# A smaller descriptor scratch for dynamic DMAs in an attention and mixture-of-experts kernel

## Chip, core and metric

The kernel runs on one core of one Trainium2 chip. The metric is the time of one execution in device microseconds (us). Times of several runs are given as the median with the lowest and highest.

## What is computed

The reference chains three parts:

```python
scores = scale * q @ k.T                      # 4 batches, 8 heads, 576 tokens, 64 wide
attn = (scores * Dmat) @ v                    # Dmat: gamma[h] ** (i - j) for i >= j, else 0
x = attn as [2304 tokens, 512]
# layer 1: top-1 mixture of 8 experts, each with room for `capacity` tokens
e = argmax(x @ w_gate); g = softmax(x @ w_gate)[e]
x2 = g * (relu(x @ w1[e]) @ w2[e])            # 512 -> 1024 -> 512; 0 where the expert is full
# layer 2: only tokens with x2 @ w_skip > 0 go through a second mixture of 8 experts
out = x2 + (g2 * (relu(x2 @ w1b[e2]) @ w2b[e2]) if x2 @ w_skip > 0 else 0)
```

All data is float32.

## The kernel before

Attention runs first, in 20 units (4 batches, 4 pairs of heads and one unit for the tail of each batch). Its output is written to a table of rows `xd` in device memory, 128 tokens at a time, by plain transfers issued from ScalarE. Routing (argmax, gate, rank of each token in its expert) is done on VectorE and TensorE while attention still runs.

The two expert layers each go through nine positions: eight experts in order of their size, the largest split in two. A position has a fixed number of token slots (`CAPS`), in tiles of 128. For each position `gather_rows` (line 838) fetches the token rows into SBUF by an indirect transfer per tile of 128 rows, from `xd` in layer 1 and from `x2d` in layer 2. `transposes` (line 704) turns them with TensorE into tiles named x_0T to x_8T, and eight steps of matmuls follow (`s1`, lines 727 to 734; `s2`, lines 753 to 768). Weights come by plain transfers from SyncE, in quarters of an expert, and where a position has more than 192 slots ScalarE (line 673) and VectorE (line 674) split them into a high and a low part.

After a position `post1` or `post2` turns the result back into rows. Layer 1 writes the rows to `x2d` (plain, from ScalarE) and scatters those that skip layer 2 to `out` (`scatter`, line 845); layer 2 scatters all its rows to `out`, adding the gathered row on VectorE (line 914). Rows of empty slots get an index beyond the table and are left out. GpSimd issues every gather and every scatter, and nothing else that is dynamic; its instructions stand in an order written out by hand: `run` asks for the gather of position p + 2 in step 6 of position p, and the scatters of a position come after it. The first gathers of a layer can't come so early, since their indices or rows are not ready.

The memory of a stage is given out in pools that are opened and closed in the code: those for attention close before the ones that only the expert layers need (`gr` for gathered rows, `xp`, `yp`) are opened. [...]

## Times and profile before

| | |
|---|---|
| median of 3 runs | 584.06 us (583.22 to 586.92) |
| the profiled execution | 584.51 us, its span 582.6 us |
| mean granted TensorE clock | 0.982 of full speed |
| TensorE matmuls / weight loads busy | 550.9 us / 513.8 us |
| VectorE, ScalarE, GpSimd busy | 309.7, 226.3, 144.8 us |
| DMA | 116.20 MB in 116085 packets |

The profile is one execution of the program. Its span is the time from the first to the last instruction; the time of the execution is 1.9 us longer. An engine's busy time is the sum over its instructions. L838 means line 838 of the kernel. PE is TensorE, PEld its weight loads, DVE VectorE, ACT ScalarE, POOL GpSimd, SP SyncE; a q behind an engine is its sequencer. [...]

### The profile page before, as it was taken

What the parts mean: (1) busy time and instruction counts of PE and PEld (TensorE: products, weight loads), DVE (VectorE), ACT (ScalarE), POOL (GpSimd) and SP (SyncE); (2) the same over time, 40 slices, a digit from 0 to 9 for tenths busy, and PEclk for the clock granted to TensorE, in tenths of its full rate; (3) what the DMA queues carried; (4) which work ended last, traced back from release to release, by engine and by line L of the source; (5) the groups of instructions that cost most, each with busy time, mean ns of one, the idle gap of its engine ahead of it and who ended that gap; (6) DMA issues with size and microseconds to landing.
All of it is one profiled execution on the core that took longest, in us unless ns stands there. A gap on an engine that the chain in (4) does not pass through costs nothing.

```text
span 582.6 us, 12184 instructions
## 1 busy us (share of the span) xinstructions
PE 550.9 (95%) x4545; PEld 513.8 (88%) x4545; DVE 309.7 (53%) x926; ACT 226.3 (39%) x457; POOL 144.8 (25%) x192
## 2 busy tenths in 40 slices
PE   5999989999899999999999999879999999999991
PEld 5989879788899999999999999768998999999980
DVE  4767889445365756767676767695556201110110
ACT  2343444413444545455455555534443222112110
POOL 4355362012221140405040304050204112210110
PEclk7899999999999999999999999989999999999997
DMA  8869786187875474655465556367646378788860
GB/s 193 188 177 252 200 252 241 42 270 224 285 258 195 155 244 156 206 176 187 162 215 154 187 169 206 123 199 232 220 129 204 131 247 257 224 278 262 259 210 9
DMA packets 116085, 116.20 MB, mean 199 GB/s; under 512 B 47654, under 2 KB 88870, under 8 KB 116018
## 3 DMA queue, kind: packets, MB, share of 16 engines
q1 hardware_dynamic: 104432, 90.12, 50.8%
q0 software_dynamic: 6320, 15.74, 8.4%
q10 hardware_dynamic: 5266, 9.48, 4.4%
q8 instruction: 38, 0.62, 0.4%
q14 instruction: 29, 0.24, 0.1%
HBM read 101.11 MB, written 17.92 MB: 204 GB/s over the span
## 4 chain that ended last, share of the span: by engine, by line
PE 81%; DVE 8%; DMA 5%; SPq 1%; issue 1%; POOL 1%; ACT 1%; POOLq 0%; DVEq 0%
PE h L727 10%; PE y L763 9%; PE h L732 6%; PE h L734 6%; PE h L733 6%; PE y L767 6%; PE y L768 5%; PE y L766 5%; PE S L187 3%; PE O L229 3%; PE O L223 2%; PE yr L797 2%; PE y L755 1%; PE Tk L170 1%; PE y L756 1%; PE y L757 1%
## 5 line engine op out<-in xcount | busy, mean ns | idle before, releaser
L674 DVE TENSOR_TENSOR lo<-r,hi 128x1024 fp32r<-128x1024 f32 x80 | 97.9, 1224 | 65.2 <-ACT hi L673 63.3
L673 ACT CAST hi<-r 128x1024 fp32r<-128x1024 f32 x80 | 83.9, 1049 | 66.2 <-PE y L767 28.3
L767 PE MATMUL y<-hl,hi 128*128 128x316 f32 (+7 forms) x256 | 76.4, 300 | 0.9 <-DVE hl L738 0.8
L768 PE MATMUL y<-hh,lo 128*128 128x316 f32 (+7 forms) x256 | 75.9, 298 | 0.0
L766 PE MATMUL y<-hh,hi 128*128 128x316 f32 (+7 forms) x256 | 73.3, 298 | 0.0
L763 PE MATMUL y<-hh,r 128*128 128x168 f32 (+3 forms) x448 | 71.6, 302 | 1.6 <-ACT hh L729 1.6
L763 PEld LDWEIGHTS y<-hh,r 128*128 128x128 f32 x448 | 64.6, 190 | 2.0 <-ACT hh L729 1.8
L737 ACT ACTIVATE hh<-h 128x240 fp32r<-128x240 f32 (+8 forms) x80 | 32.1, 401 | 71.9 <-PE h L734 70.1
L785 DVE COPY yt<-y 128x168 f32<-128x168 f32 (+11 forms) x30 | 11.8, 395 | 89.0 <-ACT yt L787 64.4
L729 ACT ACTIVATE hh<-h 128x168 f32<-128x168 f32 (+4 forms) x64 | 19.3, 302 | 95.7 <-PE h L727 95.4
L845 POOL DMA_INDIRECT out<-o,six x18 | 19.2, 1065 | 144.7 <-DVE o L914 142.6
L738 DVE SCALAR_TENSOR_TENSOR hl<-h,hh 128x240 fp32r<-128x240 f32 (+8 forms) x80 | 35.4, 443 | 31.6 <-ACT hh L737 31.6
L767 PEld LDWEIGHTS y<-hl,hi 128*128 128x128 f32 x256 | 48.2, 188 | 2.1 <-DVE hl L738 1.9
L768 PEld LDWEIGHTS y<-hh,lo 128*128 128x128 f32 x256 | 48.2, 188 | 0.0
L766 PEld LDWEIGHTS y<-hh,hi 128*128 128x128 f32 x256 | 47.1, 188 | 0.1
L845 POOL DMA_INDIRECT out<-x2r,si x24 | 27.8, 1158 | 10.4 <-issue 6.0
L190 DVE TENSOR_TENSOR P<-S,tab 128x512 f32<-128x512 f32 (+1 forms) x40 | 23.7, 631 | 11.2 <-PE S L187 10.9
L838 POOL DMA_INDIRECT g<-xd,gix x20 | 23.9, 1194 | 9.4 <-issue 5.8
L154 POOL TENSOR_TENSOR vh<-v,tab 128x512 f32<-128x512 f32 x15 | 16.2, 1082 | 26.3 <-PE O L229 17.2
L207 DVE TENSOR_TENSOR st<-st,kv 64x64 f32<-64x64 f32 x96 | 20.9, 218 | 3.0
L797 PE MATMUL yr<-ident,yt 128*128 128x128 f32 (+11 forms) x148 | 21.9, 280 | 0.5 <-DVE o L914 0.5
L187 PE MATMUL S<-qT,kT 64*128 64x128 f32 x288 | 22.4, 295 | 0.0
(757 smaller groups left out, 1288.4 us busy)
## 6 DMA issues: line engine op xcount, KB each, us to landing
r<-w1a SPq DMA_DIRECT2D x36, 512.0 KB, 4.8
r<-w2a SPq DMA_DIRECT2D x36, 512.0 KB, 4.0
r<-w1b SPq DMA_DIRECT2D x36, 512.0 KB, 5.5
r<-w2b SPq DMA_DIRECT2D x36, 512.0 KB, 4.0
xd<-xr ACTq DMA_DIRECT2D x18, 256.0 KB, 3.9
k<-k SPq DMA_DIRECT2D x32, 128.0 KB, 3.3
q<-q SPq DMA_DIRECT2D x16, 256.0 KB, 3.8
v<-v SPq DMA_DIRECT2D x32, 128.0 KB, 4.1
```

Source lines behind the costliest of these rows:

```text
L187: nc.tensor.matmul(S[hh][:, c], s.kT[hp, cs], s.qT[hp, cs], start=True, stop=True)
L673: nc.scalar.copy(hi, raw)
L674: nc.vector.tensor_sub(lo, raw, hi.bitcast(F32))
L727: nc.tensor.matmul(ps, w.r1[:, c, fc], s.xh[:, c, 0:C], start=(c == 0), stop=(c == 3))
L732: nc.tensor.matmul(ps, w.hi1[:, c, fc], s.xh[:, c, 0:C], start=(c == 0), stop=False)
L733: nc.tensor.matmul(ps, w.hi1[:, c, fc], s.xl[:, c, 0:C], start=False, stop=False)
L738: nc.vector.scalar_tensor_tensor(out=s.hl[f], in0=ps, scalar=0.0, in1=s.hh[f].bitcast(F32), op0=ALU.max, op1=ALU.subtract)
L763: nc.tensor.matmul(y, w.r2[:, f % 2, dc], s.hh[f], start=a, stop=o)
L766: nc.tensor.matmul(y, wh, s.hh[f], start=a, stop=False)
L767: nc.tensor.matmul(y, wh, s.hl[f], start=False, stop=False)
L768: nc.tensor.matmul(y, wl, s.hh[f], start=False, stop=o)
L845: r = g.nc.gpsimd.indirect_dma_start(out=g.oa["out"][:, :], out_offset=IndirectOffsetOnAxis(ap=idx, axis=0), in_=rows, in_offset=None, bou ...
```

## The change

The program is built with an explicit size of the scratch for descriptors, 4096 bytes a partition. Nothing else is touched.

```diff
-    nc = bacc.Bacc("TRN2", target_bir_lowering=False, num_devices=1)
+    nc = bacc.Bacc("TRN2", target_bir_lowering=False, num_devices=1, dynamic_dma_scratch_size=4096)
```

## Rows read from the trace of the kernel before

**Rows 1.** The page's first part: busy us, share of the span, instructions.
```profile
PE 550.9 (95%) x4545; PEld 513.8 (88%) x4545; DVE 309.7 (53%) x926; ACT 226.3 (39%) x457; POOL 144.8 (25%) x192
```

**Rows 2.** The chain of waits that ended last, shares by engine.
```profile
PE 81%; DVE 8%; DMA 5%; SPq 1%; issue 1%; POOL 1%; ACT 1%; POOLq 0%; DVEq 0%
```

**Rows 3.** TensorE's waits: for what, us in total, times, longest us.
```profile
PE s8I L466 <- DVE s8B L460: 3.0, 1, 3.0
...
PE x_1T L704 <- DMA g<-xd,fx: 1.7, 1, 1.7
...
PE x_0T L704 <- DMA g<-x2d,fx: 0.9, 1, 0.9
```

**Rows 4.** DMA queues: packets, MB, share of 16 engines; the software queue.
```profile
q0 software_dynamic: 6320, 15.74, 8.4%
```

**Rows 5.** Groups of GpSimd's instructions: count | busy us, mean ns | idle before.
```profile
L845 POOL DMA_INDIRECT out<-x2r,si x24 | 27.8, 1158 | 10.4 <-issue 6.0 <-ACT hh L737 2.6 <-ACT hi L673 1.8
L838 POOL DMA_INDIRECT g<-xd,gix x20 | 23.9, 1194 | 9.4 <-issue 5.8 <-DVE lv1lim L558 3.6
L845 POOL DMA_INDIRECT out<-o,six x18 | 19.2, 1065 | 144.7 <-DVE o L914 142.6 <-issue 2.1
L838 POOL DMA_INDIRECT g<-x2d,gix x16 | 17.8, 1110 | 6.8 <-issue 3.0 <-DVE gix L593 2.2 <-PE h L727 0.6
...
L838 POOL DMA_INDIRECT g<-xd,fx x4 | 4.1, 1027 | 10.9 <-DMA r<-w1a 10.0 <-DVE fx L512 0.3 <-PE kv L199 0.3
...
L838 POOL DMA_INDIRECT g<-x2d,fx x2 | 2.2, 1113 | 0.6 <-issue 0.6
```

**Rows 6.** Tiles g (gathers), then out (scatters): issue to landing.
```profile
DMA to landing us min/median/max: 3.3/5.9/7.5
...
DMA to landing us min/median/max: 2.5/4.4/5.9
```

**Rows 7.** Timeline of GpSimd from 381 us (start, duration); then TensorE on x_1T.
```profile
381.79 1.04 POOL L845 DMA_INDIRECT out<-x2r,si  x1 [0.65 <-ACT hh L737]
...
392.50 1.20 POOL L838 DMA_INDIRECT g<-x2d,gix  x1 [0.30 <-issue]
...
L704 PE MATMUL x_1T<-ident,g x12: 271/272/273, 401.3 to 405.0; 128*128 128x128 f32 x12
```

**Rows 8.** Timeline of GpSimd around 241 us.
```profile
241.08 0.95 POOL L838 DMA_INDIRECT g<-xd,gix  x1 [0.30 <-issue]
```

**Rows 9.** Stretch up to 237.5 us: line 838 alone, then line 845 alone.
```profile
0.00:237.50 237.50, 17.67 (x16) 0.98 0.69 206
...
0.00:237.50 237.50, 10.65 (x10) 0.98 0.69 206
```

**Rows 10.** Tile x_6T from 250 us: ns min/median/max, first and last start.
```profile
L704 PEld LDWEIGHTS x_6T<-ident,g x12: 139/140/143, 266.1 to 273.7; 128*128 128x128 f32 x12
```

**Rows 11.** The chain in order of time (start, us), from 356 us.
```profile
356.26 1.73 POOL out L845
...
358.29 1.25 POOL g L838
...
359.85 7.46 DMA g<-x2d,fx
```

**Rows 12.** Line 674 alone: ns min/median/max, first and last start.
```profile
L674 DVE TENSOR_TENSOR lo<-r,hi x80: 1211/1225/1255, 152.9 to 453.0; 128x1024 fp32r<-128x1024 f32 x80
```

**Rows 13.** The chain in order of time, from 120 us.
```profile
120.93 3.34 DMA r<-w1a
...
124.33 1.02 POOL g L838
...
125.66 5.67 DMA g<-xd,fx
```

**Rows 14.** The chain's last piece.
```profile
571.91 0.72 POOL out L845
```

## Prediction

> **What bounds the kernel now.** I read the page from the top. The engines' busy times come first: TensorE is busy for 95% of the span, GpSimd, the engine whose transfers use the scratch, for 25% [rows 1]. The chain of waits, followed back from the last instruction, says the same from the other side: 81% of it is TensorE, 5% transfers and 1% GpSimd [rows 2]. So the change can cost time only where GpSimd's transfers hold TensorE up. The list of TensorE's own waits shows where they do: 1.7 us at x_1T and 0.9 us at x_0T, both for a gathered tile; its other long wait, 3.0 us at s8I, is for VectorE [rows 3].
>
> Next I looked for what uses the scratch. The table of queues has one software queue, q0, with 6320 packets and 15.74 MB [rows 4]. The groups of GpSimd's instructions give its transfers: 24 + 20 + 18 + 16 + 4 + 2 = 84, half gathers (line 838) and half scatters (line 845), each about 1.0 to 1.2 us of GpSimd [rows 5]. The plain loads and stores go through the other queues. The last question is how many of the 84 are under way at once. A gather lands 3.3 to 7.5 us after its issue, median 5.9; a scatter 2.5 to 5.9, median 4.4 [rows 6]. The densest stretch has seven transfers, the first at 381.79 and the last at 392.50 [rows 7]: 10.7 us apart, more than the longest landing, so six at most are open at a time.
>
> **The change part by part.** Nothing is removed from or added to the instruction streams: no instruction, transfer or wait of the kernel is named in the diff. Three things can follow.
>
> *Less room for descriptors.* Before, no row shows GpSimd waiting for room. Such a wait could only stand inside a transfer's own duration or in the gap before it, and that gap is 0.30 us for transfer after transfer [rows 7, 8]. The longest transfers of a gather's group average 1.19 us [rows 5]. What room for one transfer costs is in no row, so I bound the wait. Below it is 0, the transfer meets free room. A gain is excluded, since there is no wait for room to take away. Above, it waits until the transfer ahead of it has landed, 5.9 us by the median gather. I take 0: at most six transfers are open at once, the others have landed, and what they used is free for anybody who looks.
>
> [...]
>
> For scale, take the 29th transfer in order of time. There are 16 gathers and 10 scatters before 237.5 us [rows 9], then three gathers, the last at 241.08 [rows 8]. If that one waited the full 5.9 us it would be issued at 247 and land at 253 to 254.5. TensorE first reads x_6T, the tile transposed from that group, at 266.1 [rows 10], so 11 us or more of cover remain and the price on the path is 0. Behind it on GpSimd's queue stands only the clearing of a small tile. The gathers of the later layers are likewise issued a position ahead. The tightest that TensorE does not already wait for is in the dense stretch, two scatters and then five gathers, of which the first three feed x_1T, read at 401.3 [rows 7]: the third of them is issued before the last at 392.50, and at 5.9 us lands by 398.4 at the latest.
>
> *Bookkeeping when the scratch comes round.* Even with room, GpSimd may have to look up what has finished. Lower end 0. For the upper end I take the nearest row, one more gap of 0.30 us before each transfer [rows 8]. [...] On the path are the scatter at 356.26 and the two gathers behind it, and the last scatter of all [rows 11, 14]: 4 x 0.30 = 1.2 us. I take 0 and keep 1.2 for the range.
>
> *Tiles lie elsewhere.* The reserved part of each partition shrinks, so tiles may lie at other addresses. The nearest row is the subtraction at line 674: 80 times over rotating buffers at several addresses, 1211 to 1255 ns, median 1225 [rows 12]. If addresses alone made that spread, the worst would be 30 ns x 80 = 2.4 us of VectorE in either direction, on an engine 53% busy [rows 1]. I take 0.
>
> **The sum.** The profiled execution took 584.51 us, its span of 582.6 and 1.9 around it. Added terms 0 + 0 + 0 leave 584.5 for it; it stands 0.45 above the median of the three runs, 584.06, so for a median I say 584.1.
>
> **The rivals.**
>
> *Drains.* GpSimd might wait, when it needs room, until everything issued before has landed. It matters at one place above all: the scatter at 356.26, the gathers at 358.29 and 359.85, and TensorE idle for the last of them until 367.31 [rows 3, 11]. One drain before the second gather moves it from 359.85 to 358.29 + 5.9 = 364.2: 4.3 us, all on the path, 588.4. If room came only by a drain before each transfer, the first gather would go at 356.26 + 4.4 = 360.7 and the second at 366.6, 6.7 us late. The pair at 124.33 and 125.66 [rows 13] would lose 124.33 + 5.9 - 125.66 = 4.6. The dense stretch's third gather would be issued at 381.79 + 4.4 + 4.4 + 5.9 + 5.9 = 402.4 and land at 408.3, 7.0 after TensorE wants it. Together 18.3 us, 602.4. It decides, that is, passes 1% (5.8 us), from two successive drains at 356 to 360 on. For it: a small scratch has to be given back somehow, and no row of before shows how. Against: with six open at most, older transfers have long landed and their room can be given back without a wait.
>
> *Different placement.* More free room could let the expert layers' buffers lie where no attention tile was. The gather at 124.33 is released 3.34 us into a piece of the chain that the profile puts down to a transfer [rows 13]; without it the time is 584.1 - 3.4 = 580.7. If the order of instructions shifted too and s8I's 3.0 us went [rows 3], 577.7. For it: that release follows the end of attention. Against: the stages' pools are opened and closed by the code in the same order, so everything should move together by the same amount, and the tile may equally have waited for its rows in memory.
>
> *No smaller scratch in effect.* If the size is rounded or ignored, the time is 584.1 again; only the instructions' durations around a used-up scratch would tell that case from mine.
>
> **How the numbers follow.** No effect on the path: 0.72. Not in effect: 0.07. One drain on the path, 588.4: 0.06. Drains throughout, 602.4: 0.07. Placement, 580.7: 0.04; with the order, 577.7: 0.04. A measurement of this kernel can tell about 1% from no change, its three runs spreading from 583.22 to 586.92. So within 1%: 0.72 + 0.07 + 0.06 + 0.04 = 0.89; slower 0.07; faster 0.04. The range takes in the runs' spread, 0.84 below the median doubled to 582.4, and above it 586.92 + 1.2 or the single drain, 588.5. Left out are 0.07 + 0.04 + 0.04 = 0.15.
>
> **What would show it.** Right: the same 84 transfers on q0, TensorE's waits at x_1T and x_0T unchanged within a microsecond, and the gaps of 0.30 us. Wrong: a GpSimd transfer of 3 us or more, or a long gap charged to nothing, from about the 29th on, above all before 358.29 or 359.85, with x_0T's wait grown by as much. Another order of instructions on any engine would make the placement rival likelier.

## The result, and the profile after

The changed kernel takes 579.07 us (median of 4 runs, 578.24 to 580.84); the kernel before, with one run more, 585.45 us (583.22 to 586.92). The ratio on record is 0.9912, interval 0.9887 to 0.9938 (the two medians alone give 0.989): faster by 0.9%. I had forecast no change, 584.1 us, with a range of 582.4 to 588.5.

The profiled execution took 579.04 us, its span 577.1, against 584.51 and 582.6. The instruction streams of all engines are the same in kind and order, and so is the traffic. The page's parts on the engines and on the software queue, after:

```profile
PE 553.0 (96%) x4545; PEld 515.1 (89%) x4545; DVE 309.8 (54%) x926; ACT 226.3 (39%) x457; POOL 144.7 (25%) x192
...
q0 software_dynamic: 6320, 15.74, 8.2%
```

The busy times are those of [rows 1] within 0.5%, the queue that of [rows 4]. TensorE's waits of [rows 3], after:

```profile
PE s8I L466 <- DVE s8B L460: 3.0, 1, 3.0
...
PE x_1T L704 <- DMA g<-xd,fx: 1.9, 1, 1.9
...
PE x_0T L704 <- DMA g<-x2d,fx: 0.7, 1, 0.7
```

Nothing was won there. The last piece of work does not come earlier either. GpSimd's last instruction in the timeline, the final scatter, first of the kernel before and then of the changed one:

```profile
571.64 0.99 POOL L845 DMA_INDIRECT out<-o,six  x1 [11.28 <-DVE o L914]
```

```profile
572.44 0.99 POOL L845 DMA_INDIRECT out<-o,six  x1 [11.27 <-DVE o L914]
```

It ends 0.8 us later, and yet the span is 5.5 us shorter. So the gain lies behind the last piece of the chain, from its end to the end of the span: 582.6 - 572.6 = 10.0 us before, 577.1 - 573.4 = 3.7 us after. No engine counts as busy there, since what runs is sequencers' work. The view of one line shows it, with POOLq for GpSimd's sequencer and ns min/median/max: line 1250, where the conditional part begins, and line 1266, where the program closes. Of the three DRAINs of GpSimd at line 1266 the longest is meant here, and it is the first in time. Before:

```profile
L1250 POOLq EVENT_SEMAPHORE  x5: 17/17/43, 572.5 to 572.8; - x5
L1250 POOLq COMPARE_BRANCH  x1: 45/45/45, 572.0 to 572.0; - x1
L1250 POOLq INC_SWDGE_SEM  x1: 1883/1883/1883, 572.9 to 572.9; - x1
...
L1266 POOLq DRAIN  x3: 40/107/6935, 574.8 to 582.3; - x3
```

After:

```profile
L1250 POOLq INC_SWDGE_SEM  x1: 543/543/543, 573.7 to 573.7; - x1
...
L1266 SPq EVENT_SEMAPHORE  x14: 17/28/1332, 574.2 to 577.1; - x14
L1266 POOLq DRAIN  x3: 40/107/1967, 574.3 to 576.9; - x3
```

Two of GpSimd's closing instructions shrank: INC_SWDGE_SEM by 1340 ns and the DRAIN by 4968 ns, together 6.3 us. Of this the profiled pair shows 5.5 us, because the work before it ended 0.8 us later. The later end is TensorE's clock: in the stretch from 360 to 400 us the mean granted clock was 0.96 before and 0.91 after, and in it 0.61 against 0.50 from 384 to 388 us and 1.00 against 0.84 from 388 to 392. The scatter of 381.79 stands at 381.35 in the changed kernel, 0.4 us earlier; the first one behind that stretch comes at 405.73 before and 406.52 after, 0.8 us later. TensorE had been through its 3.0 us wait at s8I just ahead of it, up to 383.7 and 383.2, in both kernels. The same stretch, before and then after (columns: us, busy time and count of PE, PEld, DVE, ACT and POOL, clock, DMA share, GB/s):

```profile
360.00:400.00 40.00, 34.52 (x248) 31.14 (x248) 28.17 (x92) 17.37 (x30) 9.64 (x12) 0.96 0.58 184
```

```profile
360.00:400.00 40.00, 34.65 (x239) 31.10 (x238) 28.00 (x91) 17.37 (x30) 9.08 (x12) 0.91 0.57 181
```

The mean granted clock differs between executions, from 0.981 to 0.991 in the four runs of the changed kernel; INC_SWDGE_SEM, as the experiments show, took 543 ns in both of its profiles.

### The profile page after: what moved, and what is told of

The parts are those of the page before. It is cut to its first block, busy times and chain, and to the rows that moved or that the text cites. A ratio compares the mean times of both kernels' runs of the same rounds, so it can differ in the third digit from the quotient of the medians.

```text
span 577.1 us, 12184 instructions
## 1 busy us (share of the span) xinstructions
PE 553.0 (96%) x4545; PEld 515.1 (89%) x4545; DVE 309.8 (54%) x926; ACT 226.3 (39%) x457; POOL 144.7 (25%) x192
## 4 chain that ended last, share of the span: by engine, by line
PE 83%; DVE 8%; DMA 4%; SPq 1%; issue 1%; ACT 1%; POOL 1%; POOLq 0%; DVEq 0%
PE h L727 11%; PE y L763 9%; PE h L732 7%; PE h L734 7%; PE h L733 6%; PE y L767 6%; PE y L768 5%; PE y L766 5%; PE S L187 3%; PE O L229 3%; PE O L223 2%; PE yr L797 2%; PE y L755 1%; PE y L756 1%; PE y L757 1%; PE Tk L170 1%
```

## Experiments

Theory A: the two closing instructions take a time that grows with n, the number of indirect transfers issued and not yet given back, and a transfer is given back only when the scratch runs out of room. I call these n transfers a list; the traces show how long the instructions take, not what they do. Theory B: they take a time that grows with the size of the scratch. The two profiles can't tell them apart: the times fell to 0.29 and 0.28, and the count on the list and the size can both have fallen like that. Theory C: the gain came from other addresses of the tiles.

**Four sizes.** Each run has the line of the diff with another number, here the first:

```diff
-    nc = bacc.Bacc("TRN2", target_bir_lowering=False, num_devices=1)
+    nc = bacc.Bacc("TRN2", target_bir_lowering=False, num_devices=1, dynamic_dma_scratch_size=11264)
```

> Scratch of 11264 bytes a partition, nothing else changed from the kernel before. [...] From the two kernels so far (6935 and 1967 ns, 1883 and 543 ns) DRAIN should then take about 1.3 us and INC_SWDGE_SEM about 0.4 us, and the time is 579, that of the changed kernel. Theory B (they take a time that grows with the size of the scratch): DRAIN 4.9 us, INC_SWDGE_SEM 1.3 us, time 582. Theory C (the gain came from tiles at other addresses): the closing instructions as before, 6.9 and 1.9 us.

> Scratch of 12288 bytes a partition, nothing else changed from the kernel before. [...] Theory B (by the size of the scratch): DRAIN 5.3 us, INC_SWDGE_SEM 1.4 us, time about 2 us below before. [...]

> Scratch of 7168 bytes a partition, nothing else changed. Theory A: 49 transfers fit, the scratch runs out near the 50th and once only, about 42 are left at the end: DRAIN 3.6 us, INC_SWDGE_SEM 1.0 us, longer than with the larger scratch of 11264 bytes; time about 580.5. Theory B (by size): DRAIN 3.2 us, INC_SWDGE_SEM 0.9 us, shorter than with 11264 bytes. The order of the two runs decides, not the small difference of the sizes.

> [...] Theory A: at the end about 7 are left, DRAIN 0.9 us, INC_SWDGE_SEM 0.25 us; the end is then set by the landing of the last scatter, as it nearly is with 4096 bytes, so no further gain at the end. Theory B (by size): DRAIN 0.7 us, INC_SWDGE_SEM 0.2 us. What giving back room costs on the way is open: if it is free, the time is 579; if each costs the 1.6 us that the 30th transfer of the changed kernel seems to have lost, about 77 x 1.6 = 123 us of GpSimd, of which the groups of transfers ahead of x_1T and x_0T lose 2 to 5 x 1.6 on the path, and the time is 585 to 600.

11264 bytes: 585.95 us, ratio 1.0011 (0.9983 to 1.0038). 12288 bytes: 584.34 us, 0.9996 (0.9970 to 1.0021). 7168 bytes: 580.0 us, 0.9919 (0.9893 to 0.9946). 1024 bytes: 579.4 us, 0.9918 (0.9891 to 0.9944). The closing of the first, then of the third and the fourth:

```profile
L1250 POOLq INC_SWDGE_SEM  x1: 1883/1883/1883, 575.3 to 575.3; - x1
...
L1266 POOLq DRAIN  x3: 40/107/6935, 577.2 to 584.7; - x3
```

```profile
L1250 POOLq INC_SWDGE_SEM  x1: 963/963/963, 574.8 to 574.8; - x1
...
L1266 POOLq DRAIN  x3: 40/107/3178, 575.8 to 579.6; - x3
```

```profile
L1250 POOLq INC_SWDGE_SEM  x1: 363/363/363, 573.4 to 573.4; - x1
...
L1266 SPq EVENT_SEMAPHORE  x14: 17/28/2652, 573.7 to 577.9; - x14
L1266 POOLq DRAIN  x3: 40/107/2920, 573.8 to 577.7; - x3
```

With 12288 bytes the two are 1883 and 6935 ns again. So the size as such does nothing between 11264 bytes and the default: B falls. B's figures took a size for the default that no run shows; it falls without them. If these sizes move the tiles as well, it is worth nothing, as neither kernel is faster than the one before: C falls. But my count for A missed as well. With 11264 bytes A was to close in 1.3 and 0.4 us, at a time of 579; that took a size of one transfer which no run shows. By the unchanged close the scratch did not run out, and so 7168 bytes closed sooner than 11264, the order that I had expected of B. Sixteen of the scatters have fewer than 128 rows; that these take less room, and that the 84 then just fit in 11264 bytes, was my estimate and not shown. It gave the next test.

**Sixty-four bytes less, more transfers, and a repeat.** The extra gathers are added in `post2`, where GpSimd has idle time; the default size stays. The first of the two kernels is shown, the second has `range(7)`:

```diff
             scatter(g, col(g.si2, 2, pos, k, n), o[0:n])
+        if 1 <= pos <= 6:
+            for j in range(3):
+                t = g.cp.tile([128, 8], F32, name=f"ex{pos}_{j}")
+                nc.gpsimd.indirect_dma_start(out=t, out_offset=None, in_=g.ia["wg1"][:, :], in_offset=IndirectOffsetOnAxis(ap=exi, axis=0))
...
+    exi = g.cp.tile([128, 1], I32, name="exi")
+    v_.tensor_copy(exi, g.rid[:, 0:1])
```

> Scratch of 11200 bytes a partition, 64 less than the run with 11264, in which the closing instructions were as before. Theory A, mended: INC_SWDGE_SEM took 1883, 963, 543 and 363 ns so far, which is 203 + 20 n with n = 84, 38, 17 and 8 transfers not yet given back. [...] Then the scratch runs out at the 84th transfer, 8 are left, INC_SWDGE_SEM takes about 363 ns and DRAIN ends with the landing of the last scatter; the time is 579. Theory B', that there is some step of size between 7168 and 11264 bytes that has nothing to do with the count: nothing changes over 64 bytes unless the step happens to lie there, 1883 and 6935 ns, 584.5.

> Default scratch, and 18 gathers more (128 rows of 32 bytes each into tiles that nobody reads, three after the scatters of each of positions 1 to 6 of layer 2, issued by GpSimd where it idles). Theory A: n = 102, so INC_SWDGE_SEM takes 203 + 20 x 102 = 2243 ns and DRAIN, at the 82 ns a transfer between 84 and 38 of them, 8.4 us; the end comes 1.8 us later than before, time about 586. Theory B (size alone): 1883 and 6935 ns, time as before.

> [...] Theory A: the default scratch too runs out, near the 120th transfer, about 14 are left, INC_SWDGE_SEM takes about 203 + 20 x 14 = 483 ns, DRAIN about 1.2 to 2.9 us with the landing of the last scatter, and the kernel ends sooner with half as many transfers more: about 579, if the extra gathers (42 x 1.3 = 55 us of GpSimd) stay hidden beside TensorE; up to 5 us more if they delay gathers. Theory B (size alone): 1883 and 6935 ns, 584.5 or more. The number of transfers alone, without giving back: 203 + 20 x 126 = 2723 ns and 10.4 us, 588.

> The changed kernel once more, for its time beside the others of this call and for one open point: in its first profile the 30th transfer took 2.03 us where it took 1.05 before and was issued late as well. If giving back 21 transfers costs GpSimd 80 ns each there, the same 1.6 us appear again at the 30th transfer; if it was chance, its duration is 1.05 again. INC_SWDGE_SEM 543 ns and DRAIN about 2 us either way.

With 11200 bytes, 64 fewer than the run that changed nothing: 580.45 us, ratio 0.9906 (0.9875 to 0.9936).

```profile
L1250 POOLq INC_SWDGE_SEM  x1: 363/363/363, 576.6 to 576.6; - x1
...
L1266 SPq EVENT_SEMAPHORE  x14: 17/28/1645, 576.9 to 580.1; - x14
L1266 POOLq DRAIN  x3: 40/107/1912, 577.0 to 579.9; - x3
```

INC_SWDGE_SEM took 363 ns with 1024 bytes too. By A the 84th transfer, the last of all, runs out of room, and that is enough to shorten the list to what 1024 bytes leave. Of the theories only a count puts a step of 5 us between two sizes 64 bytes apart. If the 84 fit in 11264 bytes and not in 11200, one takes 11200 / 84 to 11264 / 84, 133 to 134 bytes in the mean: an estimate from these two runs.

The two kernels with more transfers and the default scratch, first 18 more, then 42 more:

```profile
L1256 POOLq INC_SWDGE_SEM  x1: 2248/2248/2248, 581.8 to 581.8; - x1
...
L1272 POOLq DRAIN  x3: 40/107/8405, 584.1 to 593.1; - x3
```

```profile
L1256 POOLq INC_SWDGE_SEM  x1: 488/488/488, 616.5 to 616.5; - x1
...
L1272 POOLq DRAIN  x3: 40/107/1218, 617.0 to 618.8; - x3
```

18 more lengthen the close as A said (2243 ns and 8.4 us expected); 42 more shorten it below that of the changed kernel, as A said of a default scratch that now runs out too: with 84, 102 and 126 transfers INC_SWDGE_SEM took 1883, 2248 and 488 ns. The size of the default is shown by no run, and so my 120th transfer is not either.

The times did not come as I expected: 593.69 us, ratio 1.0131 (1.0091 to 1.0172), and 618.91 us, 1.0559 (1.0523 to 1.0596). The extra gathers did not stay beside the work as I had expected. With 42 more, TensorE waits 17.3 us for ScalarE's hh and 10.5 us on nothing shown:

```profile
PE y L763 <- ACT hh L729: 17.3, 4, 5.7
PE y L763 <- issue: 10.5, 3, 5.2
```

What ScalarE waited for there was not followed further. With 18 more, the last scatter comes 6.5 us later (578.16), 1.8 us are the longer close, and 2.4 us lie between GpSimd's branch and its next instruction, of which more below. These two runs tell of the closing instructions; as a way to a better time they fail.

The changed kernel again: 581.14 us, ratio 0.9909 (0.9878 to 0.9940), INC_SWDGE_SEM 543 ns as before. The 30th transfer, in the first profile of the changed kernel, in the second, and in the kernel before:

```profile
264.76 2.03 POOL L845 DMA_INDIRECT out<-x2r,si  x1 [1.28 <-ACT hh L737]
```

```profile
265.92 2.02 POOL L845 DMA_INDIRECT out<-x2r,si  x1 [1.28 <-ACT hh L737]
```

```profile
264.41 1.05 POOL L845 DMA_INDIRECT out<-x2r,si  x1 [0.66 <-issue]
```

It starts 0.62 us later behind its predecessor and takes 0.98 us more: 1.6 us in both, so not chance, and one transfer before the 31st, where by the mean of 133 to 134 bytes 4096 bytes first run out. The longer duration alone would prove little: ten transfers of the kernel before take 1.7 to 2.0 us with a scratch that by A never runs out, and the 22nd, for one, takes 1.87 us there and 0.97 in the second run of the changed kernel. One of the ten, before:

```profile
439.82 2.02 POOL L845 DMA_INDIRECT out<-o,six  x1 [0.30 <-DVE o L914]
```

The 1.6 us cost nothing, since the gathers behind that transfer, the last issued at 272.99, are first read at 296.2. The same step is not visible everywhere that room ran out. With 11200 bytes the 84th transfer starts 1.1 us late; with 7168 bytes, which by the same mean run out at the 54th, that one takes 1.88 us against 1.91 before and is not late; with 1024 bytes one scatter, the 57th, takes 3.00 us against 0.98. What giving back costs, and when, stays open; that it is small against the 6.3 us is shown by 1024 bytes, where by the same mean nearly every transfer from the eighth on must get room and the time is the same 579.

**Fewer transfers, with both sizes.** The scatters of layer 1 are left out, so `out` lacks the rows of the tokens that skip layer 2:

```diff
-        for k, (n, xr) in enumerate(xs):
-            scatter(g, si[0:n, k:k + 1], xr[0:n])
```

> Default scratch, the 24 scatters of layer 1 left out (rows of tokens that skip layer 2 are not written to out), 60 transfers in all. Theory A: n = 60, so INC_SWDGE_SEM takes 203 + 20 x 60 = 1403 ns and DRAIN 73 + 81.7 x 60 = 4.98 us: the closing instructions are 2.4 us shorter than before, and the time is about 583 beside 585.5 if nothing else on the path feels the missing scatters (GpSimd holds gathers behind them, so 1 to 2 us more may go). Theory B (size of the scratch): 1883 and 6935 ns, and only what the missing scatters give on the way.

> The same 60 transfers with a scratch of 4096 bytes. Theory A: the scratch runs out near the 29th and the 50th transfer, 18 are left, INC_SWDGE_SEM takes 563 ns and DRAIN 1.5 us or until just after the last landing; against the run with 60 transfers and the default scratch the gain is what is between the two closings, at most (1403 + 4975) - (563 + 1540) = 4.3 us, or 4 with the landing of the last scatter in the way: less than the 6 us that the same size gave with 84 transfers. Theory B: 543 and about 2000 ns as with 84 transfers, and the same gain of 6 us.

Closing with the default scratch, then with 4096 bytes:

```profile
L1248 POOLq EVENT_SEMAPHORE  x5: 17/17/43, 575.2 to 575.6; - x5
L1248 POOLq COMPARE_BRANCH  x1: 53/53/53, 572.3 to 572.3; - x1
L1248 POOLq INC_SWDGE_SEM  x1: 1403/1403/1403, 575.6 to 575.6; - x1
...
L1264 POOLq DRAIN  x3: 40/107/4975, 577.1 to 582.6; - x3
```

```profile
L1248 POOLq COMPARE_BRANCH  x1: 53/53/53, 570.9 to 570.9; - x1
L1248 POOLq INC_SWDGE_SEM  x1: 563/563/563, 574.3 to 574.3; - x1
...
L1264 POOLq DRAIN  x3: 40/107/1545, 574.9 to 577.0; - x3
```

The closing instructions come out as expected (1403 ns and 4.98 us; 563 ns and 1.5 us). The time of the first does not: 584.91 us, ratio 0.9991 (0.9973 to 1.0009), where 2.4 us less were due. The rows show where they went: from GpSimd's COMPARE_BRANCH to its next instruction 572.3 to 575.2, 2.9 us, where the kernel before has 572.0 to 572.5. The same 2.9 to 3.0 us stand in the other kernels with other instruction counts (578.5 to 581.4 with 18 more). Why a branch takes longer there was not tried. Between the two kernels with 60 transfers it cancels: 579.44 us, 0.9908 (0.9888 to 0.9928), against 584.91, so 5.5 us, of which the closing instructions are (1403 + 4975) - (563 + 1545) = 4.3; in the profiles the last scatter also comes 1.4 us earlier, 570.6 against 572.0.

**What the runs give together.** The number of transfers is known in three runs where by A the scratch never ran out, 60, 84 and 102. DRAIN: (6935 - 4975) / 24 = 81.67 ns and (8405 - 6935) / 18 = 81.67 ns a transfer; INC_SWDGE_SEM: 480 / 24 = 20.0 and 365 / 18 = 20.3 ns. So INC_SWDGE_SEM = 203 + 20 n, up to 5 ns more in the table, and DRAIN = 75 + 81.67 n, and the other runs can be read backwards:

| scratch, transfers | INC_SWDGE_SEM ns | n from it | DRAIN by n, ns | DRAIN ns | time us |
|---|---|---|---|---|---|
| default, 84 | 1883 | 84 | 6935 | 6935 | 585.45 |
| 12288, 84 | 1883 | 84 | 6935 | 6935 | 584.34 |
| 11264, 84 | 1883 | 84 | 6935 | 6935 | 585.95 |
| 11200, 84 | 363 | 8 | 728 | 1912 | 580.45 |
| 7168, 84 | 963 | 38 | 3178 | 3178 | 580.0 |
| 4096, 84 | 543 | 17 | 1463 | 1967 and 2829 | 579.07 and 581.14 |
| 1024, 84 | 363 | 8 | 728 | 2920 | 579.4 |
| default, 102 | 2248 | 102 | 8405 | 8405 | 593.69 |
| default, 126 | 488 | 14 | 1218 | 1218 | 618.91 |
| default, 60 | 1403 | 60 | 4975 | 4975 | 584.91 |
| 4096, 60 | 563 | 18 | 1545 | 1545 | 579.44 |

The times belong to four groups of runs, in which the kernel before took 584.2 to 585.8 us.

Where n is read backwards, DRAIN can say whether it is a count. In three runs to which the lines are not fitted, the n of INC_SWDGE_SEM gives DRAIN to the nanosecond: 38, 14 and 18 for 3178, 1218 and 1545. What brings n there can only be estimated, by the mean of 133 to 134 bytes. Suppose that all but the newest seven transfers are given back each time; the seven are fitted to 11200 bytes, where 8 are left after the 84th. Then 7168 bytes run out at the 54th transfer and leave 84 - 46 = 38, the value of the table; with 1024 bytes, where hardly more than seven fit at all, it has 8. For 4096 bytes the mean is too coarse: with 23 given back at the 31st, 54th and 77th it leaves 84 - 69 = 15 and, with 60 transfers, 60 - 46 = 14, where the table has 17 and 18. The seven are an inference from these runs; no trace shows the giving back itself.

Three kernels, in four profiles, have a DRAIN longer than n says. In each the end goes with the last scatter's landing: in the changed kernel SyncE's wait at line 1266, which its profile puts down to that scatter's transfer, ends at 575.5 and GpSimd's DRAIN at 576.3. With 1024 bytes SyncE's longest wait, from 573.7 on, is 2652 ns and ends at 576.3, and the DRAIN, from 573.8 on, ends at 576.7; with 11200 bytes the two end at 578.5 and 578.9. That is the floor: where the branch takes 0.5 us and n is 8 or 17, the landing is later than the close, and the smaller scratch of 1024 bytes gains no more (579.4 us). No version here beats the changed kernel.

## Why the prediction was wrong

**The step that failed** is the first bound, "A gain is excluded, since there is no wait for room to take away." I priced the scratch by what GpSimd might wait for while the kernel works, and put the close at nothing without a reason. In that close INC_SWDGE_SEM and DRAIN took 1883 and 6935 ns before, 543 and 1967 ns after. The row was there to be asked for: the chain's last piece ends at 571.91 + 0.72 = 572.6 [rows 14], the span at 582.6, and I took the 10.0 us between as given. GpSimd's 25% and 1% of the chain [rows 1, 2] don't hold them either, as a sequencer's DRAIN is not busy time. All the kernel's gain, 6.3 us of instructions, lies in that stretch.

**What held.** The instruction streams are unchanged. Gathers on the path lost nothing: x_1T waits 1.9 us, x_0T 0.7 us, within 0.2 of [rows 3]. The scratch was used up at the 30th transfer, as far as its late start shows, one later than the 29th. That 29th rests on a size of one transfer that no run shows, and so do the counts in my expectations (49 and 42, 77, the 120th, the 29th and 50th); what the runs show in their place is the 30th transfer late by 1.6 us and an INC_SWDGE_SEM that stands for 38, 8, 14 and 18 transfers left. Nor does any run show that room is free as soon as its transfer has landed, which I had taken for granted. The price of 0 on the path held: the 1.6 us at the 30th transfer are hidden. Other addresses, if the tiles moved, are worth nothing, as [rows 12] suggested: 585.95 and 584.34 us with 11264 and 12288 bytes. So the signs that I had named for being right came true, and the forecast was wrong all the same: none of them looked behind the last piece of the chain.

**The rivals.** Drains on the path, 588.4 or 602.4 us, did not come, and even 1024 bytes, by the mean of 133 to 134 an estimated seven transfers, leave the time at 579.4. Placement, 580.7 or 577.7 us, came close to the measured time for the wrong reason; the runs with 11264 and 12288 bytes rule it out. None of my cases had the mechanism that acted, so its 0.08 of faster time was not foresight.

## What to carry to other kernels

Compare the end of the chain of waits with the end of the span before any sum: what lies between is worth as much per microsecond as anything on the path, and the view of the closing line shows it. A resource that is only freed when it runs out, as A has it of this one, leaves its clean-up for the end; here each indirect transfer still on the list cost 0.1 us (20 and 81.67 ns) of a close that nothing hid. In a kernel that issues many such transfers, a scratch that runs out shortly before the end may take most of the list away where other work covers it; it did here, and no other kernel was tried.

## What the runs showed of the hardware

- INC_SWDGE_SEM took 203 + 20 n ns (up to 5 ns more) and DRAIN 75 + 81.67 n ns, n from 14 to 102, where no landing came later.
- The same DRAIN took 6935 ns with 11264 bytes and 1912 ns with 11200; by A the last transfer still finds room in the one and not in the other.
- The n of INC_SWDGE_SEM gave DRAIN to the nanosecond in three kernels to which the lines are not fitted (38, 14 and 18). That the list is cut to its newest seven is an estimate: fitted to 8, it gives the 38; for 17 and 18 it is too coarse, and for 14 no run shows the size.
- With 4096 bytes the 30th transfer was 1.6 us late (2.03 us instead of 1.05, and 0.62 behind), twice alike; with 11200 bytes 1.1 us, with 7168 nothing to be seen.
- GpSimd's branch at the end took 0.5 us to the next instruction in the kernel before and 2.9 to 3.0 us in kernels with another number of instructions; the cause is open.
